# A constant of -0.5 is stored in 32 bytes of each partition in place of 256, which moves the tiles behind it by 224 bytes

## The chip, the cores and the metric

The kernel runs on one core of one Trainium2 chip. The metric is device time in microseconds (us) of one execution; the time before is 712.57 us, the median of three runs that lie between 712.51 and 714.41 us.

## What is computed

Three stages follow each other, all in float32 results:

```python
kv  = einsum('bhsd,bhse->bhde', k, v)              # linear attention, B=4, H=8, S=576, D=64
out = einsum('bhsd,bhde->bhse', q, kv)
out = out / sqrt(mean(out*out, -1) + 1e-6) * g_norm
x   = out as (2304, 512)                           # tokens x (heads * 64)
x   = ((x @ w_a) * (x @ w_b)) @ w_out              # 512 -> 1536 -> 512
h   = x @ w_in                                     # 512 -> 1024
e   = exp(h - max(h)); solu = h * e / (sum(e) + 1e-9)
ln  = (solu - mean(solu)) / sqrt(var(solu) + 1e-6) * g_ln
y   = ln @ w_out2                                  # 1024 -> 512
```

The weights of the second and third stage arrive as float64 and are taken apart into float32 pieces on the chip.

## The kernel before, in words

All large products use the float32r type, and each of them is made of three matmuls: a high part and a low part of either factor, without low times low. The helper `three` (L702) issues them: L703 high by high, L704 with the moving factor's low part, L705 with the stationary factor's low part. Each matmul is preceded on TensorE by a load of its 128x128 stationary block, which the profile shows as an LDWEIGHTS under PEld; here the load of the next block starts beside the matmul that still runs. In this text "weights" are the stationary operand that is loaded in that way, and "moving" is the operand of 512, 384, 256 or 128 columns that streams past it.

There are four kinds of large products, with these tiles:

- **ab** (L703 to L705, called from `ab_items`): stationary `wh`/`wl` (pieces of w_a and w_b), moving `xh`/`xl` (the attention's output, transposed). 12 slices of 128 of the 1536 columns, each over 5 blocks of tokens: two blocks of 384 and three of 512. Per slice and block there are 24 matmuls, so 12 x 3 x 24 = 864 matmuls of 512 columns and 12 x 2 x 24 = 576 of 384 columns.
- **y** (L788, `y_items`): stationary `wh`/`wl` of w_out, moving `gh`/`gl`, the product of the two halves of ab. 432 matmuls of 512 columns, 288 of 384. ab and y alternate, block by block.
- **h** (L928, `run_h`): stationary `lateh`, and moving `wd` or `latel`, the pieces of w_in, by a scheme with seven products in place of eight. 378 matmuls of 512 columns.
- **out** (L703 to L705, `run_o`): stationary `dh` (high) and `dl` (low), moving `wh_o`/`wl_o`. The low part `dl` has no tile of its own: it lies in the back of `lateh` for every second tile of tokens and in the back of `latel` for the others. Of the eight pairs of weight tiles six lie in the ring of `wh`/`wl`, and two in `latel`. 17 of the 18 tiles of tokens are whole: 17 x 24 = 408 matmuls of 512 columns; the last one is cut into halves of 256.

Transposes (L680, L1020) and the attention's own products (L590, L597, L635) are the remaining work on TensorE. h and out of different tiles alternate in the last 200 us.

The order of the work on every engine is fixed when the program is built. The class `Order` plays the program through with fixed costs for each operation, and emits an instruction where its model says that it is due. The engines then run their lists and wait for each other by semaphores.

SBUF is filled from two sides, by pools that are stacked up. From the left: the pool `cst` (the tiles `ident`, `gn`, `gl_sb` and `mhalf`, L184 to L187), then `xs` (`xh0`, `xl0`, `xh1`, `xl1`, and in their places later `lateh` and `latel`), then `att` (`bd`, `kv`, `tail`, `q`, `qs`, `x`, `sq`, `r`), and after the attention in its place `w2` (`wd`, `bt`). From the right: `wp` (the ring of `wh`/`wl`), `yp` (`ya`), and `ph1` (`raw`, `u`, `f`, `a`, `gh`, `gl`), replaced at the end by `ph2` (`u`, `st`, `dh`, `ot`). Every tile but the small ones has a size that is a multiple of 256 bytes in each partition, so the small ones decide at which remainder modulo 256 the others begin.

`mhalf` holds the exponent -0.5. GpSimd fills it once (L189) and reads it in two places, where it raises a variance to that power: 8 columns at L662, one column at L992.

As the program before is laid out, the places in each partition are, in bytes:

| tiles | from | remainder modulo 256 |
| --- | --- | --- |
| `ident`; `mhalf` | 16512; 17088 | 128; 192 |
| `xh0`, `xl0`, `xh1`, `xl1`, later `lateh`, `latel` | 17344 to 91072 | 192 |
| `bd`, `kv`, `tail`, `q`, `qs`, `x`, later `wd`, `bt` | 91072 to 136128 | 192 |
| `raw`, `f`, `a`, `gh`, `gl`, `ya`, later `dh`, `ot` | 137184 to 204768 | 224 |
| `u` of the last stage | 138656 to 155040 | 160 |
| `wh`/`wl`, later `wh_o`/`wl_o` | 204768 to 229344 | 224 |

Slices within a tile begin at multiples of 256 bytes, so these remainders hold for the operands of the float32r matmuls too.

Of the kernel before, what the change touches and what calls it, by code (L numbers as in the profile page):

```python
# [9 lines left out]
F32 = mybir.dt.float32  # L10
# [7 lines left out]
P = 128  # L18
B, H, S, D = 4, 8, 576, 64
# [119 lines left out]
def attention_moe_moe_kernel(ctx: ExitStack, tc, kv_in, kv_tail, q_in, g_norm, w1, w_in, w_out2, g_ln, out):  # L139
# [6 lines left out]
    cst = ctx.enter_context(tc.tile_pool(name="cst", bufs=1, side="left"))  # L146
# [37 lines left out]
    ident = cst.tile([P, P], F32, tag="ident", name="ident")  # L184
    gn = cst.tile([P, 1], F32, tag="gn", name="gn")
    gl_sb = cst.tile([P, NF2], F32, tag="gln", name="gln")
    mhalf = cst.tile([P, 8 * H], F32, tag="mhalf", name="mhalf")  # L187

    nc.gpsimd.memset(mhalf, -0.5)  # L189
    bds = [att.tile([P, NP, P], F32, tag=f"bd{n}", name=f"bd{n}", bufs=1) for n in range(2)]  # L190
# [1038 lines left out]
```

## Time and profile before

| what | value |
| --- | --- |
| median of three runs | 712.57 us |
| time of the profiled execution | 712.37 us |
| its span, first to last instruction | 710.6 us |
| TensorE matmul (PE) busy | 697.0 us, 98% |
| TensorE weight loads (PEld) busy | 600.5 us, 85% |
| VectorE (DVE) busy | 513.6 us, 72% |
| ScalarE (ACT), GpSimd (POOL) busy | 261.9 us, 247.6 us |
| HBM traffic | 60.8 MB, 86 GB/s on average |

The profiled execution is 0.2 us shorter than the median, and lies 1.8 us above its own span. A matmul's record holds its latency too: consecutive records overlap, so a busy share of 98% doesn't say that TensorE runs at its peak. What a matmul costs in a stream is read from the distance between the starts of two that follow each other.

### The profile page before, as it was taken

To read this page: it belongs to the slowest core of one execution; us is meant where nothing else is said; L and a number is where in the kernel's file an instruction comes from. 1 tells how busy PE (TensorE), PEld (TensorE's weight loads), DVE (VectorE), ACT (ScalarE), POOL (GpSimd) and SP (SyncE) were. 2 spreads that over 40 slices of the span, in tenths; PEclk is the share of its full clock that TensorE was granted. 3 is DMA by queue.
4 is the path that set the end of the run, shared out by engine and by line. 5 is a ranking of instruction groups with operands and counts; after the bars stand their busy time and mean duration, and the time that the engine had idled before them with its cause. 6 is when DMAs were issued, how large, how long until landed. Compare 5 with 4: busy or idle time off the path is not lost.

```text
span 710.6 us, 9627 instructions
## 1 busy us (share of the span) xinstructions
PE 697.0 (98%) x3690; PEld 600.5 (85%) x3690; DVE 513.6 (72%) x746; ACT 261.9 (37%) x462; POOL 247.6 (35%) x243
## 2 busy tenths in 40 slices
PE   5899999999999999999999999999999999999998
PEld 5799888989898888888898989898778888888887
DVE  2989735888978899689878788554597857765560
ACT  3787534333233233232232232212354434343231
POOL 2766314332374445513232322202335433322110
PEclk9999999999999999999999999999999999999999
DMA  8984101122242121132232312013500000000001
GB/s 292 372 273 132 60 0 60 60 101 78 89 151 86 60 89 60 55 104 80 90 119 88 119 61 90 30 60 123 203 0 30 16 30 31 16 23 23 30 30 45
DMA packets 23630, 61.45 MB, mean 86 GB/s; under 512 B 4768, under 2 KB 6048, under 8 KB 23584
## 3 DMA queue, kind: packets, MB, share of 16 engines
q1 hardware_dynamic: 23584, 60.83, 24.4%
q8 instruction: 29, 0.48, 0.3%
q14 instruction: 17, 0.14, 0.1%
HBM read 48.76 MB, written 12.06 MB: 86 GB/s over the span
## 4 chain that ended last, share of the span: by engine, by line
PE 97%; DMA 1%; DVE 1%; ACT 0%; SPq 0%; issue 0%; ACTq 0%
PE y L788 21%; PE ab L703 14%; PE ab L704 14%; PE ab L705 14%; PE h L928 12%; PE out L705 5%; PE out L703 5%; PE out L704 5%; PE o L635 3%; PE t L1020 2%; PE t L680 1%; PE pkv L590 1%; DMA kv<-in_kv 1%; SPq L263 0%; PE pkv L597 0%
## 5 line engine op out<-in xcount | busy, mean ns | idle before, releaser
L703 PE MATMUL ab<-xh,wh_w 128*128 128x512 f32 (+1 forms) x480 | 179.8, 375 | 0.0
L704 PE MATMUL ab<-xl,wh_w 128*128 128x512 f32 (+1 forms) x480 | 178.5, 372 | 0.0
L705 PE MATMUL ab<-xh,wl_w 128*128 128x512 f32 (+1 forms) x480 | 178.5, 372 | 0.0
L801 DVE TENSOR_TENSOR ya<-y,ya 128x1024 f32<-128x1024 f32 (+1 forms) x110 | 122.2, 1111 | 2.1 <-PE y L788 1.8
L757 ACT COPY a<-ab 128x512 f32<-128x512 f32 (+1 forms) x60 | 32.7, 545 | 197.8 <-PE ab L705 197.7
L424 POOL TENSOR_TENSOR f_w<-f_w,wh_w 128x512 f32<-128x512 f32 x36 | 47.9, 1330 | 165.5 <-ACT wh_w L423 112.6
L758 DVE TENSOR_TENSOR ab<-ab,a 128x512 f32<-128x512 f32 (+1 forms) x60 | 38.7, 645 | 89.1 <-ACT a L757 89.0
L703 PEld LDWEIGHTS ab<-xh,wh_w 128*128 128x128 f32 x480 | 90.2, 188 | 13.5 <-issue 0.3
L705 PEld LDWEIGHTS ab<-xh,wl_w 128*128 128x128 f32 x480 | 90.2, 188 | 13.0
L704 PEld LDWEIGHTS ab<-xl,wh_w 128*128 128x128 f32 x480 | 90.2, 188 | 12.7
L788 PE MATMUL y<-gh,wh_w 128*128 128x512 f32 (+1 forms) x240 | 89.2, 372 | 0.0
L788 PE MATMUL y<-gl,wh_w 128*128 128x512 f32 (+1 forms) x240 | 88.6, 369 | 0.3 <-DVE gl L760 0.3
L788 PE MATMUL y<-gh,wl_w 128*128 128x512 f32 (+1 forms) x240 | 88.5, 369 | 0.0
L928 PE MATMUL h<-wd,lateh 128*128 128x512 f32 x216 | 58.2, 390 | 0.0
L788 PEld LDWEIGHTS y<-gl,wh_w 128*128 128x128 f32 x240 | 45.1, 188 | 6.6 <-DVE gl L760 0.8
L788 PEld LDWEIGHTS y<-gh,wh_w 128*128 128x128 f32 x240 | 45.1, 188 | 6.1
L788 PEld LDWEIGHTS y<-gh,wl_w 128*128 128x128 f32 x240 | 45.0, 188 | 5.8
L425 POOL TENSOR_TENSOR wl_w<-f_w,u_w 128x512 fp32r<-128x512 f32 x36 | 47.7, 1328 | 3.6 <-DVE u_w L345 2.1
L928 PEld LDWEIGHTS h<-wd,lateh 128*128 128x128 f32 x216 | 40.5, 188 | 8.5
L928 PE MATMUL h<-latel,lateh 128*128 128x512 f32 x162 | 46.4, 394 | 0.0
L703 PE MATMUL out<-wh_o,dh 128*128 128x512 f32 (+1 forms) x114 | 44.1, 387 | 0.0
L875 POOL TENSOR_TENSOR lateh<-ya,lateh 128x512 fp32r<-128x512 f32 (+1 forms) x18 | 18.2, 1016 | 73.9 <-ACT lateh L874 73.9
(103 smaller groups left out, 1142.3 us busy)
## 6 DMA issues: line engine op xcount, KB each, us to landing
raw_w<-in_w SPq DMA_DIRECT2D x36, 512.0 KB, 3.3
kv<-in_kv SPq DMA_DIRECT2D x16, 512.0 KB, 7.1
out<-ot SPq DMA_DIRECT2D x17, 256.0 KB, 2.0
raw_i<-in_w_in SPq DMA_DIRECT2D x8, 512.0 KB, 3.3
raw_o<-in_w_out SPq DMA_DIRECT2D x8, 512.0 KB, 3.3
so<-raw_o SPq DMA_DIRECT2D x8, 512.0 KB, 2.7
q<-in_q SPq DMA_DIRECT2D x12, 256.0 KB, 5.3
si<-wd SPq DMA_DIRECT2D x6, 512.0 KB, 2.6
```

The costliest lines, as they stand in the source:

```text
L424: ("T", 1.32, lambda: nc.gpsimd.tensor_tensor(out=f, in0=f, in1=hi.bitcast(F32), op=ALU.subtract)),
L425: ("T", 1.38, lambda: nc.gpsimd.tensor_tensor(out=lo, in0=f, in1=u, op=ALU.add)),
L635: nc.tensor.matmul(ps[m * w:(m + 1) * w, p * P:(p + 1) * P], lhsT=src[:, m * w:(m + 1) * w], rhs=bds[b % 2][:, p], start=True, stop=True)
L703: nc.tensor.matmul(o, lhsT=ah, rhs=bh, start=first, stop=False)
L704: nc.tensor.matmul(o, lhsT=ah, rhs=bl, start=False, stop=False)
L705: nc.tensor.matmul(o, lhsT=al, rhs=bh, start=False, stop=last)
L757: ("A", 0.45 * k, lambda: nc.scalar.copy(out=a, in_=ps[:, 0, 0:nb])),
L758: ("V", 0.54 * k, lambda: nc.vector.tensor_tensor(out=g, in0=g, in1=a, op=ALU.mult)),
L788: nc.tensor.matmul(o, lhsT=x[:, s], rhs=y, start=f == fs[0] and n == 0, stop=f == fs[-1] and n == 2)
L801: op = ("V", 0.9 * nb / NB, lambda: nc.vector.tensor_tensor(out=dst, in0=src, in1=dst, op=ALU.add))
L875: ("G", 2.15 * cost, lambda: nc.gpsimd.tensor_tensor(out=lo[:, n], in0=src, in1=hi[:, n].bitcast(F32), op=ALU.subtract)),
L928: nc.tensor.matmul(o, lhsT=x, rhs=y, start=first and k == m == 0, stop=k == 1 and m == 2, skip_group_check=not first)
```

## The change

Only the allocation of `mhalf` changes:

```diff
-    mhalf = cst.tile([P, 8 * H], F32, tag="mhalf", name="mhalf")
+    mhalf = cst.tile([P, H], F32, tag="mhalf", name="mhalf")
```

H is 8: 64 float32 values per partition become 8. The instructions and their order stay the same on every engine, but for the one fill at L189, which writes 128x8 in place of 128x64. Everything that is stacked on the left behind `mhalf` begins 224 bytes earlier: `xh`, `xl`, `lateh`, `latel`, `bd`, `kv`, `tail`, `q`, `qs`, `x`, `wd` and `bt` begin at remainder 224 in place of 192. What is stacked from the right stays where it was, and so does `ident`.

## Rows read from the trace of the kernel before

**Rows 1.** The page, busy time by engine: us, share of the span, instructions.

```profile
PE 697.0 (98%) x3690; PEld 600.5 (85%) x3690; DVE 513.6 (72%) x746; ACT 261.9 (37%) x462; POOL 247.6 (35%) x243
```

**Rows 2.** The page, the chain that ended last, by engine.

```profile
PE 97%; DMA 1%; DVE 1%; ACT 0%; SPq 0%; issue 0%; ACTq 0%
```

**Rows 3.** Waits of PE: who waited for whom, total us, times, longest.

```profile
PE pkv L590 <- DMA kv<-in_kv: 7.0, 3, 5.7
PE t L680 <- DVE r L657: 2.1, 1, 2.1
...
PE y L788 <- DVE gl L760: 0.3, 1, 0.3
```

**Rows 4.** Busy us (count) of PE, PEld, DVE, ACT, POOL, then PEclk, DMA share, GB/s.

```profile
200.00:300.00 100.00, 100.00 (x487) 88.30 (x486) 84.39 (x118) 32.01 (x58) 51.95 (x39) 1.00 0.22 74
```

**Rows 5.** Timeline of PE, ab of 512 columns, then y: start, us, instruction.

```profile
299.54 0.40 PE L705 MATMUL ab<-xh,wl_w 128*128 128x512 f32 x1
...
300.23 0.40 PE L705 MATMUL ab<-xh,wl_w 128*128 128x512 f32 x1
300.47 0.40 PE L703 MATMUL ab<-xh,wh_w 128*128 128x512 f32 x1
...
302.57 0.40 PE L788 MATMUL y<-gh,wh_w 128*128 128x512 f32 x1
302.80 0.39 PE L788 MATMUL y<-gl,wh_w 128*128 128x512 f32 x1
...
305.29 0.40 PE L703 MATMUL ab<-xh,wh_w 128*128 128x512 f32 x1
```

**Rows 6.** The chain piece by piece, 600 to 625 us: start, us, what.

```profile
599.99 9.55 PE h L928 x42
...
615.11 0.87 PE t L1020 x8
```

**Rows 7.** Timeline of PE in out, two tiles of tokens.

```profile
594.79 0.39 PE L703 MATMUL out<-wh_o,dh 128*128 128x512 f32 x1
...
598.95 0.27 PE L1020 MATMUL t<-ident,u 128*128 128x128 f32 x1
...
609.37 0.39 PE L703 MATMUL out<-wh_o,dh 128*128 128x512 f32 x1
...
614.95 1.03 PE L1020 MATMUL t<-ident,u 128*128 128x128 f32 x8
```

**Rows 8.** Timeline of PE, ab of 384 columns, then y of 384.

```profile
283.01 0.34 PE L703 MATMUL ab<-xh,wh_w 128*128 128x384 f32 x1
...
287.17 0.34 PE L788 MATMUL y<-gh,wh_w 128*128 128x384 f32 x1
...
288.24 0.33 PE L788 MATMUL y<-gh,wh_w 128*128 128x384 f32 x1
...
289.28 0.39 PE L703 MATMUL ab<-xh,wh_w 128*128 128x512 f32 x1
```

**Rows 9.** Timeline of all engines, the first 6 us.

```profile
0.72 0.15 POOL L189 MEMSET mhalf<- 128x64 f32 x1 [0.29 <-POOLq L1219]
0.72 0.39 SPq L263 DMA_DIRECT2D raw_w<-in_w  x1
...
1.16 0.42 SPq L263 DMA_DIRECT2D kv<-in_kv  x1
...
4.47 0.66 ACT L324 ACTIVATE u_w<-raw_w 128x512 f32<-128x512 f32 x1 [2.47 <-DMA raw_w<-in_w]
...
5.74 1.12 PE L590 MATMUL pkv<-kv 128*64 128x64 f32 x16 [5.74 <-DMA kv<-in_kv]
```

**Rows 10.** Groups of POOL by form: count, busy us, mean ns, idle before.

```profile
L425 POOL TENSOR_TENSOR wl_w<-f_w,u_w 128x512 fp32r<-128x512 f32 x36 | 47.7, 1328 | 3.6 <-DVE u_w L345 2.1
L461 POOL TENSOR_TENSOR wd<-bt,wd 128x512 fp32r<-128x512 f32 x14 | 18.7, 1339 | 11.8 <-ACT wd L460 8.7 <-issue 3.1
```

## Prediction, before the change was run

> **What bounds the kernel now.** I read the page's busy times first: TensorE's matmuls are busy for 98% of the span, every other engine for 72% or less [rows 1]. That alone doesn't make TensorE the bound, since its records overlap. So I went on to the chain that ended last, which runs on PE for 97% [rows 2], and to PE's waits [rows 3]: 7.0 us for the first `kv` transfers, 2.1 us once for a statistic, 0.3 us once for `gl`. The first two belong to the attention; behind it TensorE waits for practically nobody, and a nanosecond less per matmul is a nanosecond less at the end. The question is therefore what a matmul costs in its stream, and the timeline tells that by the distance of starts. The same 512 columns cost two different amounts, at the same granted clock (1.00 from 200 to 300 us, the upper of the two levels, 2.4 GHz) [rows 4]:
>
> - ab: 13 starts from 299.54 to 302.57 us, 233.1 ns each [rows 5].
> - y: 11 starts from 302.80 to 305.29 us, 226.4 ns each [rows 5].
> - h: 42 in 9.55 us, 227.4 ns each [rows 6].
> - out: 18 from 594.79 to 598.95 us, 231.1 ns each; 24 from 609.37 to 614.95 us, 232.5 ns each [rows 7].
>
> Set beside the table of places, this has an order. In y the moving tile and the weights both begin at remainder 224, in h both at 192: the two cheap ones. In ab the moving tile begins at 192 and the weights at 224: dear. In out the three matmuls of a group mix both: `dh` and `wh_o` at 224, `dl` at 192; dear on average. So 192 by itself is cheap and 224 by itself is cheap, and what goes with the 5 to 7 ns is that the two streams which TensorE reads side by side begin at different remainders. After the change all of them begin at 224.
>
> **The change, part by part.** The sum is made against the profiled execution, 712.37 us, 0.2 us under the median of the runs.
>
> ab of 512 columns. 864 matmuls, now 233.1 ns. What one takes with equal remainders is bounded by y (226.4) and h (227.4); I take the middle, 226.9, since both hold for an undisturbed stream. 864 x 6.2 ns = 5.4 us less. Ends: 864 x (233.1 - 227.4) = 4.9 and 864 x (233.1 - 226.4) = 5.8 us.
>
> out of 512 columns. 408 matmuls, now 231.8 ns as the mean of the two tiles shown. 408 x (231.8 - 226.9) = 2.0 us less. Ends: 408 x (231.1 - 227.4) = 1.5 and 408 x (232.5 - 226.4) = 2.5 us. The last tile's halves of 256 columns: no row tells the two cases apart there, and 24 x 2 x 6 ns would be 0.3 us; taken as nothing.
>
> ab of 384 columns. 576 matmuls at (287.17 - 283.01) / 24 = 173.3 ns [rows 8]. y of 384 columns, with equal remainders, takes 178.3 ns in its first six and 173.3 ns in its last six, (288.24 - 287.17) / 6 and (289.28 - 288.24) / 6. At 384 columns the unequal pair costs nothing visible, so I take no gain. Ends: ab settles at y's mean of 175.8 ns, 576 x 2.5 = 1.4 us more; or the six slower ones in y are an after-effect of the ab before them and vanish, 288 x 2.5 = 0.7 us less.
>
> h and y stay pairs of equal remainders: nothing. The transposes keep unequal ones (`ident` at 128, `u` at 160), and at 0.87 us for eight, 109 ns each, nothing changes for them [rows 6]. The attention's own products read two tiles of the left side, which move together: nothing.
>
> Transfers into the moved tiles (`kv`, `tail`, `q`, `qs`, the late weights) now land at 224. A transfer of the same size lands there already: the first `raw_w` goes from its issue at 0.72 us to its first reader at 4.47 us, 3.75 us; the first `kv`, at 192, from 1.16 to 5.74 us, 4.58 us, behind it in the same queue [rows 9]. Nothing says that 224 is the slower landing place. Of the 0.83 us between the two, 0.44 us is the later issue; I take zero, with the other 0.4 us to either side for the wait at the start, which is on the path.
>
> The other engines' work on moved tiles. GpSimd subtracts 128x512 in 1339 ns where its operands begin at 192 (`wd`, `bt`) and in 1328 ns where they begin at 224 (`wl_w`, `f_w`) [rows 10]: nothing, and it lies beside TensorE's work in any case. The fill of `mhalf` is 0.15 us at 0.72 us [rows 9], 5 us before TensorE's first matmul; its cover is the wait for `kv`, and without that cover it would give 0.1 us.
>
> Does another engine become late? From 200 to 300 us VectorE is busy for 84.39 us [rows 4]. Over the 660 us from the attention's first part to the end TensorE gets 1.1% faster, so VectorE would stand at some 85.3: it remains below. Late next would be `gl`, for which TensorE waited 0.3 us in one place [rows 3].
>
> Sum: 5.4 + 2.0 = 7.4 us less, 705.0 us, and with the 0.2 us to the median 705.2; I say 705.4, since a switch from one kind of matmul to another has its own small steps (the first y start after ab is still 0.23 us apart [rows 5]). Ends: 4.9 + 1.5 - 1.4 - 0.4 = 4.6 and 5.8 + 2.5 + 0.7 + 0.4 = 9.4 us less, so with the 0.2 us 703.2 to 708.0.
>
> A rule that speaks against this. The rows say that ab and out are dearer, and not why. The Trainium skill, "TensorE: Matmul & The Clock Gate", in the part "Step-by-step: what each phase is for", says that TensorE has two independent SBUF read ports and that loading the next tile's weights doesn't steal read bandwidth from the matmul that runs. By that rule the place of one operand couldn't matter to the other, and the sum would be 0 in place of 7.4 us. No row of this trace shows the ports; the rows at 384 columns agree with it, those at 512 don't refute it while the first rival below stands.
>
> **The rivals.**
>
> *No change: it is not the remainder.* Every pair that is unequal here is also a pair that reaches across SBUF: in y both tiles are stacked from the right, above 137184 bytes, in h both from the left, below 136128; in ab one of each. A cost of reaching across would give the same rows, and the change doesn't touch it. Against it: distance by itself isn't dear, since h reads weights at 17344 and moving tiles up to 123840 bytes at 227.4 ns. And starts in ab that lie 0.24 us apart where the mean is 0.233 [rows 5] look more like two streams that slip against each other than like a fixed surcharge. For it: 384 columns cross SBUF at no cost, but are unequal at no cost as well, which speaks against both alike. Time: 712.6 us, the median.
>
> *Half the gain.* In out only one of three weight loads is unequal to what moves beside it, and yet the whole group is dear. Something that lasts, or another cause, may hold part of the 6 ns. Half of 7.4 us less than the median: 708.9 us.
>
> *Slower.* The only 384-column matmuls above 173.3 ns are six of twelve in y, and those have equal remainders [rows 8]. If equal starts make two reads meet at that length, and 512 columns gain nothing because the first rival holds there, all 576 ab matmuls of 384 go from 173.3 to 178.3 ns: 2.9 us more, 715.5 us. It ends on that side of what can be told as long as the 512-column matmuls give back less than 0.8 us. Against it: the other six of the same twelve, with the same tiles, take 173.3 ns.
>
> That the change wouldn't do what it says is excluded by the layout: all float32r operands do begin at 224.
>
> **How the numbers follow.** The forecast gets 0.71: two cheap cases at two different remainders and two dear ones at a difference of 32 bytes is more than a coincidence of places would have to give. Half the gain gets 0.09, no change 0.14, slower 0.06. A difference of 0.3%, 2.1 us, is about what a measurement of this kernel can tell from none: faster is then 0.71 + 0.09 = 0.80, the same 0.14, slower 0.06. The range holds the forecast and half the gain: from 703.2 us, the far end of the sum, to 710.0 us, a good microsecond above half the gain. The forecast's own range is 703.2 to 708.0 us.
>
> **What would show it.** Right: starts in ab and in out 226 to 228 ns apart at 512 columns, by the timeline; h and y as before; ab of 384 at 173 ns; PE's waits as before, and its share of the chain still 97%. Wrong: ab still at 233 ns (the remainder isn't the cause); ab at 384 columns at 176 ns or more (the third rival); a longer wait for `kv` at the start (the landing place costs); or ab at 227 ns with the time unchanged, which would need a new wait of PE for `gl`, `a` or `wh`.

## The result, and the profile after

The changed kernel takes 706.17 us, the median of five runs between 705.72 and 706.67; the kernel before takes 712.57 us (712.47 to 714.41). The ratio is 0.9901, with a 95% interval of 0.9885 to 0.9916: faster by 1.0%, 6.4 us. The profiled execution took 706.26 us, 6.1 us less than the one of before, on a span of 704.5 us. The profiled execution of one later kernel, e5, had a mean granted clock of 0.561 and took 1160.7 us, so that its profile is of no use here and the kernel was run again as e10.

The page of the changed kernel, busy time by engine and the chain that ended last:

```profile
PE 690.4 (98%) x3690; PEld 600.5 (85%) x3690; DVE 513.3 (73%) x746; ACT 262.0 (37%) x462; POOL 247.5 (35%) x243
PE 95%; DMA 3%; SPq 0%; DVE 0%; ACT 0%; issue 0%; ACTq 0%
```

Only PE's matmuls lost time, 697.0 to 690.4 us [rows 1]; the weight loads and the other engines stand within 0.3 us of what they were. What PE waits for, in total, times and longest:

```profile
PE pkv L590 <- DMA kv<-in_kv: 7.6, 4, 5.8
PE t L680 <- DVE r L657: 2.2, 1, 2.2
PE o L635 <- ACT x L671: 0.6, 1, 0.6
PE y L788 <- DVE gl L760: 0.3, 1, 0.3
```

Against [rows 3] there is 0.6 us more for `kv` and nothing new. The timeline of PE over the part that answers to [rows 5] and [rows 8]:

```profile
278.30 0.39 PE L788 MATMUL y<-gh,wh_w 128*128 128x512 f32 x1
...
281.06 0.33 PE L703 MATMUL ab<-xh,wh_w 128*128 128x384 f32 x1
...
282.12 0.33 PE L703 MATMUL ab<-xh,wh_w 128*128 128x384 f32 x1
...
285.24 0.33 PE L788 MATMUL y<-gh,wh_w 128*128 128x384 f32 x1
...
287.32 0.39 PE L703 MATMUL ab<-xh,wh_w 128*128 128x512 f32 x1
...
294.91 0.39 PE L703 MATMUL ab<-xh,wh_w 128*128 128x512 f32 x1
...
296.99 0.39 PE L703 MATMUL ab<-xh,wh_w 128*128 128x512 f32 x1
297.22 0.39 PE L704 MATMUL ab<-xl,wh_w 128*128 128x512 f32 x1
...
300.39 0.39 PE L788 MATMUL y<-gh,wh_w 128*128 128x512 f32 x1
300.62 0.39 PE L788 MATMUL y<-gl,wh_w 128*128 128x512 f32 x1
...
303.11 0.39 PE L703 MATMUL ab<-xh,wh_w 128*128 128x512 f32 x1
```

From 297.22 to 300.39 us there are 14 starts of ab, 226.4 ns each, where it was 233.1 ns [rows 5]; y from 300.62 to 303.11 us stays at 226.4 ns. But the nine starts from 294.91 to 296.99 us, directly behind a block of 384 columns, are 231 ns apart. In the same way the first six of ab at 384 columns, behind y at 512, lie 177 ns apart (281.06 to 282.12), the next 18 173.3 ns (282.12 to 285.24). y at 384 columns behind ab at 384 takes 173.3 ns throughout (285.24 to 287.32). In the changed kernel the stream needs six to nine matmuls to settle after each change between 384 and 512 columns, and none from ab to y or back where the length stays. Before, the slow pieces lay elsewhere: ab at 384 columns behind y at 512 settled at once, and y had a slow six behind ab of the same length too [rows 8]. Nor had y at 512 columns any slow piece behind ab at 384, 12 starts in 2.72 us, where the changed kernel takes 2.76 us (278.30 to 281.06). From the timeline of the kernel before:

```profile
280.29 0.39 PE L788 MATMUL y<-gh,wh_w 128*128 128x512 f32 x1
...
283.01 0.34 PE L703 MATMUL ab<-xh,wh_w 128*128 128x384 f32 x1
```

The last stage, by the chain and by PE's timeline in out:

```profile
594.89 9.54 PE h L928 x42
```

```profile
589.76 0.39 PE L703 MATMUL out<-wh_o,dh 128*128 128x512 f32 x1
...
593.62 0.40 PE L705 MATMUL out<-latel,lateh 128*128 128x512 f32 x1
```

h is what it was, 227 ns [rows 6]; out has 17 starts in 3.86 us, 227.1 ns each, where it was 231.1 [rows 7].

To see where the time went, I added the distance from each start to the next over all float32r matmuls of the two traces. In us, before and after: ab of 512 columns 201.7 and 197.2; ab of 384 101.4 and 101.7; y of 512 99.1 and 99.1; y of 384 51.2 and 50.9; h 87.1 and 86.8; out 95.4 and 93.5, and its halves of 256 columns 5.5 and 5.6. The sum is 641.5 before and 634.9 after, 6.6 us less. The first ab matmul starts 0.4 us later, at 27.66 in place of 27.24 us: hence, to 0.1 us, the 6.1 us.

### The profile page after: what moved, and what is told of

The parts are those of the page before. It is cut to its first block, busy times and chain, and to the rows that moved or that the text cites. A ratio compares the mean times of both kernels' runs of the same rounds, so it can differ in the third digit from the quotient of the medians.

```text
span 704.5 us, 9627 instructions
## 1 busy us (share of the span) xinstructions
PE 690.4 (98%) x3690; PEld 600.5 (85%) x3690; DVE 513.3 (73%) x746; ACT 262.0 (37%) x462; POOL 247.5 (35%) x243
## 4 chain that ended last, share of the span: by engine, by line
PE 95%; DMA 3%; SPq 0%; DVE 0%; ACT 0%; issue 0%; ACTq 0%
PE y L788 21%; PE ab L703 14%; PE ab L705 14%; PE ab L704 14%; PE h L928 12%; PE out L705 5%; PE out L703 5%; PE out L704 5%; PE t L1020 2%; DMA kv<-in_kv 2%; PE o L635 2%; DMA raw_w<-in_w 1%; PE t L680 1%; PE pkv L590 1%; SPq L263 0%; DVE ya L801 0%
## 5 line engine op out<-in xcount | busy, mean ns | idle before, releaser
L703 PE MATMUL ab<-xh,wh_w 128*128 128x512 f32 (+1 forms) x480 | 177.9, 371 | 0.0
```

The costliest lines, as they stand in the source:

```text
L703: nc.tensor.matmul(o, lhsT=ah, rhs=bh, start=first, stop=False)
```

## The experiments

Theory: a matmul of 512 columns costs 5 to 7 ns more when the moving tile and the weights that are loaded beside it begin at different remainders modulo 256 bytes. Rivals: the absolute place or remainder of the left tiles (or the smaller fill), a cost of pairs that reach across SBUF, a rule on a smaller modulus. In the fences below the instruction stands at its line of that kernel's own text.

### The same remainder, elsewhere: e1

```diff
-    mhalf = cst.tile([P, H], F32, tag="mhalf", name="mhalf")
+    mhalf = cst.tile([P, 9 * H], F32, tag="mhalf", name="mhalf")
```

> The constant takes 288 bytes in place of 32, so the left tiles lie 256 bytes higher than in the change and 32 bytes higher than in the kernel before; they begin at remainder 224 as in the change, and the fill is larger than in either. Theory 'equal remainders': 706.2 us as the change, ab of 512 columns at 228 ns from start to start. Rival 'the smaller fill or the lower place did it': 712.6 us as before, ab at 233 ns.

Measured: 705.86 us, ratio to before 0.9902 (0.9875 to 0.9928). The timeline of PE, ab of 512 columns and the y behind it:

```profile
297.14 0.39 PE L703 MATMUL ab<-xh,wh_w 128*128 128x512 f32 x1
...
299.86 0.39 PE L788 MATMUL y<-gh,wh_w 128*128 128x512 f32 x1
```

12 starts of ab in 2.72 us, 226.7 ns. Neither fewer bytes nor lower addresses did it: 32 bytes more than before do the same as 224 bytes less.

### Unequal remainders on one side: e2

```diff
     xs = ctx.enter_context(tc.tile_pool(name="xs", bufs=1, side="left"))
+    padp = ctx.enter_context(tc.tile_pool(name="padp", bufs=1, side="left"))
...
+    padp.tile([P, 56], F32, tag="pad", name="pad")
```

> The change, with 224 bytes left free between the pool of xh/lateh and the pool that later holds wd and bt: wd begins at 192, lateh and latel at 224, all of them stacked from the left. Theory 'equal remainders': the h matmuls whose moving tile is wd (216) go from 226 or 227 ns to 231 to 235 ns, those with latel (162) stay but for the ones beside a wd, ab and out stay at 227; 1.3 to 2.3 us more than the change, 707.5 to 708.5 us. Rival 'only pairs that reach from the left stack to the right one cost, the change having moved them into a better place': no pair of h reaches across, h stays at 227 ns, 706.2 us.

Measured: 707.86 us, ratio 0.9928 (0.9901 to 0.9955), 2.0 us over e1, which was measured beside it. The same stretch of h, first in this kernel, then in the changed one, from PE's timelines:

```profile
595.59 0.94 PE L930 MATMUL h<-latel,lateh 128*128 128x512 f32 x3
...
597.07 0.85 PE L930 MATMUL h<-latel,lateh 128*128 128x512 f32 x3
597.75 0.86 PE L930 MATMUL h<-wd,lateh 128*128 128x512 f32 x3
598.45 0.85 PE L930 MATMUL h<-latel,lateh 128*128 128x512 f32 x3
...
605.40 0.40 PE L705 MATMUL out<-wh_o,dh 128*128 128x512 f32 x1
```

```profile
594.65 0.94 PE L928 MATMUL h<-latel,lateh 128*128 128x512 f32 x3
...
604.26 0.39 PE L703 MATMUL out<-wh_o,dh 128*128 128x512 f32 x1
```

9.81 us against 9.61. Three matmuls with `latel` take 0.68 us (597.07 to 597.75), three with `wd` 0.70 us (597.75 to 598.45), 233 ns each, as expected. h has become dear where its moving tile was shifted, and both tiles are on the left: no pair reaches across. With ab cheap across SBUF in the changed kernel, the rival of reaching across has fallen on both sides.

### Other differences: e3, e4, e6 to e9

All six change only the size of `mhalf`, here e3:

```diff
-    mhalf = cst.tile([P, H], F32, tag="mhalf", name="mhalf")
+    mhalf = cst.tile([P, 3 * H], F32, tag="mhalf", name="mhalf")
```

> The constant takes 96 bytes: left tiles at remainder 32, right ones at 224, a difference of 64 bytes upwards. Theory 'any difference modulo 256 costs': ab of 512 and out at 231 ns or more, 712 us or more. Theory 'what counts is the place within 64 bytes': both sides at 32 modulo 64, ab at 227 ns, 706.2 us.

> The constant takes 160 bytes: left tiles at remainder 96, right ones at 224, a difference of 128 bytes. Theory 'any difference modulo 256 costs': ab of 512 and out at 231 ns or more, 712 us or more, perhaps ab of 384 too. Theory 'what counts is the place within 64 or 128 bytes': ab at 227 ns, 706.2 us.

> Left tiles at remainder 0, right ones at 224: a difference of 32 bytes as before, but with the left side ahead. Theory 'the size of the difference counts': 712.6 us as before, ab of 512 at 233 ns. Rival 'it counts which stream is ahead': the moving tile of ab is now the one that is ahead, and ab stands between 227 and 231 ns, near 709 us, as at a difference of 64 the same way (709.3 us).

> Left tiles at remainder 64, right ones at 224, a difference of 96 bytes with the left side ahead. Theory 'every difference costs, those near 128 the most': 711 to 713 us, ab of 512 at 231 ns or more. Rival 'some differences are as good as none, or better': 706 us or less, ab at 227 ns or less.

> Left tiles at remainder 128, right ones at 224, a difference of 96 bytes with the right side ahead. Theory 'every difference costs': 711 to 713 us, ab of 512 at 231 ns or more. Rival 'some differences are as good as none, or better': 706 us or less, ab at 227 ns or less.

> Left tiles at remainder 160, right ones at 224, a difference of 64 bytes with the right side ahead; the last of the seven differences. Theory 'every difference costs, by no simple rule of its size': 709 to 714 us, ab of 512 at 229 ns or more. Rival '64 is cheaper than the others either way': near 709 us.

The table holds all eight differences that sizes in steps of 32 bytes allow; the difference is the left tiles' remainder less the right tiles'. The ns are mean distances of starts over the whole trace, a few stalls included; the sum is that of all float32r matmuls, as in the section on the result.

| difference | kernel | `mhalf` | median us | ab 512, ns | out 512, ns | ab 384, ns | sum us |
| --- | --- | --- | --- | --- | --- | --- | --- |
| 0 | the change | H | 706.17 | 228.2 | 229.2 | 176.6 | 634.9 |
| +32 | e6 | 2 H | 714.73 | 233.7 | 234.4 | 179.1 | 643.9 |
| +64 | e3 | 3 H | 709.28 | 229.8 | 233.0 | 175.7 | 638.0 |
| +96 | e7 | 4 H | 714.74 | 234.0 | 233.8 | 178.8 | 643.9 |
| 128 | e4 | 5 H | 712.78 | 233.5 | 233.4 | 177.9 | 641.9 |
| -96 | e8 | 6 H | 713.71 | 234.3 | 234.5 | 176.0 | 642.0 |
| -64 | e9 | 7 H | 713.42 | 233.6 | 233.3 | 179.2 | 642.8 |
| -32 | before | 8 H | 712.57 | 233.5 | 233.8 | 176.1 | 641.5 |

The groups of PE by form (count, busy us, mean ns of one record) of e3, e4, e9 and the change, in this order, bear the columns of ab out:

```profile
L704 PE MATMUL ab<-xl,wh_w 128*128 128x512 f32 x288 | 113.0, 392 | 0.0
L704 PE MATMUL ab<-xl,wh_w 128*128 128x384 f32 x192 | 64.5, 336 | 0.0
```

```profile
L704 PE MATMUL ab<-xl,wh_w 128*128 128x512 f32 x288 | 113.7, 395 | 0.0
L704 PE MATMUL ab<-xl,wh_w 128*128 128x384 f32 x192 | 64.7, 337 | 0.0
```

```profile
L704 PE MATMUL ab<-xl,wh_w 128*128 128x512 f32 x288 | 113.7, 395 | 0.0
L704 PE MATMUL ab<-xl,wh_w 128*128 128x384 f32 x192 | 65.0, 338 | 0.1
```

```profile
L704 PE MATMUL ab<-xl,wh_w 128*128 128x512 f32 x288 | 112.4, 390 | 0.0
```

At 512 columns the record's mean stands 2 ns over that of the change at +64, and 5 ns over it at 128 and -64; by the starts 1.6 of the 5.3 ns of the kernel before are left at +64. That holds for ab alone: out takes 233.0 ns there, 3.8 of its 4.6 ns. Equal remainders are the best of the eight. A smaller modulus is refuted: differences of 64 and 128 would have cost nothing. So is a larger one, by e1, whose left tiles lie 256 bytes higher than those of the change. But the theory that every difference costs alike missed too: +64 upwards costs under half of the rest, while -64 costs it all; and +32 costs 714.73 us, with a ratio of 1.0033 (1.0021 to 1.0045) slower than -32, which no theory here had. Of the times expected for the six only those of e4 and e9 came out: e3 lies between its two, e6 above both of its, e7 and e8 above 713 us. By the sums e6 and e7 stand 2.4 us over the kernel before and e9 1.3 us; ab at 384 columns adds 2.7 to 3.1 ns x 576 = 1.6 to 1.8 us in each of the three: at that length some differences cost something and others don't.

### All operands at remainder 0: e5 and e10

The change with a tile of 224 bytes allocated first on the right side, and `mhalf` of 2 H:

```diff
+    padp = ctx.enter_context(tc.tile_pool(name="padp", bufs=1, side="right"))
+    padp.tile([P, 56], F32, tag="pad", name="pad")
     wp = ctx.enter_context(tc.tile_pool(name="wp", bufs=6, side="right"))
```

> Left and right tiles are both moved, so that all float32r operands begin at remainder 0. Theory 'only the difference of the remainders counts': 706.2 us as the change, 512 columns at 226 or 227 ns in all four products. Rival 'the remainder itself counts as well, 0 being a whole line': under 705 us, 512 columns under 226 ns.

> The kernel with all float32r operands at remainder 0 once more, for its profile at the full clock. Theory 'only the difference counts': 706.2 us, starts at 512 columns 226 or 227 ns apart as at remainder 224. Rival '0 is better': under 705 us.

Measured: 706.87 us in e5, ratio 0.9908 (0.9881 to 0.9935), and 705.37 us in e10, ratio 0.9900 (0.9883 to 0.9916). In e10's timeline the y of 512 columns takes 12 starts in 2.72 us, 226.7 ns:

```profile
299.57 0.39 PE L790 MATMUL y<-gh,wh_w 128*128 128x512 f32 x1
...
302.29 0.39 PE L705 MATMUL ab<-xh,wh_w 128*128 128x512 f32 x1
```

The sum over all starts is 635.2 us, 0.3 us above that of the change. The remainder itself doesn't count, only that both sides have the same one.

### Fewer switches of length: e11, and the change again: e12

```diff
-BLOCKS = [(0, 384), (384, 384), (768, 512), (1280, 512), (1792, 512)]
+BLOCKS = [(0, 256), (256, 512), (768, 512), (1280, 512), (1792, 512)]
...
-    COST = {384: 0.52, 512: 0.68}
+    COST = {256: 0.36, 512: 0.68}
```

> The change, with the tokens cut into one block of 256 and four of 512 in place of two of 384 and three of 512. If each switch between lengths costs some 30 to 40 ns in the six to nine matmuls behind it, as the profile of the change shows, 47 switches in place of 65 give 0.6 us back, and starts at 256 columns are 118 ns apart: 705.5 us. Rival 'at 256 columns the weight load of 109 ns no longer hides, or the other engines have too little time for a short block': 707 us or more, with new waits of PE.

> The change itself once more, beside the kernel with one block of 256 on the same chip: 706.2 us, ab of 512 at 228 ns. If its first ab matmul comes at 27.2 us in place of 27.7 us, the 0.4 us later start in its first profile was of that execution, not of the landing place of the kv tiles.

Measured: 706.26 us for e11 (704.03 to 707.62, six runs) and 706.63 us for e12 (705.22 to 708.73): their ratios to before, 0.9906 (0.9889 to 0.9923) and 0.9916 (0.9900 to 0.9933), can't be told apart. In the profiles the sum over all starts is 634.2 us against 635.0, so 0.8 us came back in the streams. Where 512 columns follow 256 in e11, five starts are slow in place of the nine behind 384. The end doesn't show it, since the first ab matmul of e11 started only at 29.11 us, and PE's waits have grown:

```profile
PE pkv L590 <- DMA kv<-in_kv: 9.9, 4, 5.7
PE t L680 <- DVE r L657: 2.2, 1, 2.2
PE t L680 <- DVE xl L693: 0.8, 1, 0.8
```

How much of that late start belongs to the block of 256, and how much to this execution, wasn't separated. The first ab matmul of the change itself, with the same 224 as landing place, starts at 27.66 us in the first profile and at 28.59 us in e12's:

```profile
28.59 0.44 PE L703 MATMUL ab<-xh,wh_w 128*128 128x384 f32 x1
```

In e1 it is 27.06 us with the same remainder, in e10 26.59 us at remainder 0, in e8 29.38 us at 128. A scatter of over a microsecond at one and the same remainder says that the 0.4 us between the first two profiles need no cause in the landing place.

## Why the prediction was right, point by point

The forecast was 705.4 us and 7.2 us less; measured were 706.17 us and 6.4 us less.

- *What bounds it*: right. 6.6 us less in TensorE's streams came out as 6.1 us at the end of the profiled execution, with no new wait.
- *Equal remainders make the stream cheap*: right, and more than the profile of before could show. e1 keeps the gain with other addresses, e10 with another remainder, e2 takes part of it back with a difference on one side alone.
- *ab of 512 columns, 5.4 us*: 4.5 us. The settled stream came out as forecast, at 226.4 ns. The step that failed is the one that gave all 864 matmuls the rate of an undisturbed stream: 21 times nine of them stand behind a block of 384 columns at 231 ns, 21 x 9 x (231 - 226.5) = 0.9 us. The forecast had 0.2 us for all such switches. [rows 8] showed such a piece in y, behind ab of the same length, and I took it for an after-effect of ab's unequal pairs; that agrees with the result, since y settles at once there now. What the prediction lacked is that equal pairs have slow pieces too, behind a change of length.
- *out, 2.0 us*: 1.9 us.
- *ab of 384 columns, nothing, between 1.4 us more and 0.7 less in y*: 0.3 us more in ab, 0.3 less in y. Both ends were at work in part: y lost its slow six in the blocks behind ab of the same length and kept it behind ab of 512 columns, and ab got a slow six behind y of 512.
- *h and y nothing; out's halves nothing*: 0.2 us less in h, 0.1 us more in the halves. That y of 512 columns stayed at 99.1 us is luck: its 23 whole blocks behind ab of 512 gave back 16 ns each on average, and its 10 behind ab of 384 lost 39 ns each, 0.4 us either way.
- *Landing place, nothing with 0.4 us either way*: 0.4 us more in the one pair of profiles; by the other runs that is scatter.
- *The rivals*: "no change" fell with the result itself and with e2. "Half the gain" fell, with 6.4 of 7.4 us; its doubt, why in out one unequal load of three makes all three dear, stays open. Settling might answer it, if the unequal pair comes back before the stream has settled; but in e2 three matmuls with `latel` directly behind three unequal ones take 0.68 us, 227 ns each, and don't need six to settle. "Slower" needed ab at 384 columns to go to 178.3 ns throughout; settled it stands at 173.3.
- *The rule that spoke against*: the Trainium skill, "TensorE: Matmul & The Clock Gate", "Step-by-step: what each phase is for", has two independent read ports, so that loading weights doesn't take bandwidth from the matmul that runs. Here 512 columns take 226.4 or 233 ns by nothing but where the one operand begins relative to the other. So as far as it says that the two reads are without effect on each other, the measurement decides against it at this length; settled ab at 384 columns, 173.3 ns before and after, agrees with it, but not the means of that length at other differences, up to 179.2 ns in e9 against 176.6 at equal remainders.
- *What would show it*: the main signs came, starts in ab and out at 227 ns and ab of 384 at 173 ns once settled. Three others didn't come clean. The wait for `kv` grew by 0.6 us, named as a sign that the landing place costs; the scatter of the other runs speaks against that. Over the whole trace ab of 384 stands at 176.6 ns, past the 176 ns that were to speak for "slower"; before it was 176.1 already. The chain's share of PE fell from 97 to 95%, because the chain now goes back through the first transfers, at the start of the execution.

## What to carry to other kernels

Look at the distances of starts of matmuls of the same length, and sort them by where the moving tile and the weights begin in SBUF. Where long float32r matmuls run back to back, let both begin at the same remainder modulo 256 bytes; a small constant allocated ahead of the large tiles decides that, and a few bytes of padding are free. Try it in the profile of each length separately, since what 512 columns gain, 384 don't.

## What I had not expected of the hardware

- The surcharge has a sign and no simple rule: with the left side ahead by 64 bytes ab of 512 columns takes 229.8 ns on average, with the right side ahead by 64 bytes 233.6. Why, these runs leave open.
- A stream settles. With equal remainders six to nine matmuls are 3 to 5 ns dearer after each change between 384 and 512 columns. With unequal ones in ab it was otherwise: y had slow pieces behind ab of its own length, and none at 512 columns behind ab of 384. What decides, these runs leave open.
- At 256 columns equal remainders are the dearer ones: the last tile's halves in out take 117.5 ns from start to start before and 119.9 after, 48 matmuls and 0.1 us here.
